# A DiT attention block: the shift of channels 256 to 1151 computed as rows by column-tiled matmuls and turned by one VectorE block transpose

## The chip, the cores and the metric

The kernel runs on one core of one Trainium2 chip, in one launch. The metric is device time in microseconds (us), the median of several runs. A profiled execution stands beside it: its span is the time from the first to the last instruction, and its own time has what lies around the span as well.

## The reference

B = 2 batches of N = 256 tokens, D = 1152 channels, all arrays bf16. Cut to what matters:

```python
mod = (_silu(c) @ w_mod).reshape(B, 6, 1, D)
shift_a, scale_a, gate_a, shift_m, scale_m, gate_m = [mod[:, i] for i in range(6)]
h = _layernorm(x, axis=-1) * (1 + scale_a) + shift_a
qkv = h @ wqkv
q, k, v = ...                      # thirds of qkv
p = _softmax(jnp.einsum('bqd,bkd->bqk', q, k) * D ** (-0.5), axis=-1)
a = jnp.einsum('bqk,bkd->bqd', p, v) @ wo
return x + gate_a * a
```

Only shift_a, scale_a and gate_a are used. Each is one row of 1152 numbers per batch: silu(c), 2 x 1152, times 1152 columns of w_mod.

## The kernel before, in words

Channels and tokens. The 512 tokens of both batches (T) are handled together. h is kept transposed, with channels on partitions, in nine blocks of 128 channels: hT_sb[:, cc, :] is 128 channels by 512 tokens. The query and key projections contract over channels, so block k of hT_sb is the moving operand of the matmuls for block k, and the weights' 128 x 128 tiles are stationary. The shift is wanted in the same form: a scalar per partition for each block and batch, sh_sb[:, cc, b].

How shift and scale are made. scT_sb holds silu(c) transposed: 128 partitions by 9 blocks by 32 columns, of which two are the batches and thirty are zero. mod_mm (L489) takes, for each channel block cc, nine matmuls: a 128 x 128 tile of w_mod stationary, two columns of scT_sb moving. The result, 128 channels by 2 batches, adds up in PSUM bank 7 (ps[7]). s_mm / s_ev (L497, L500) do this for the scale by the groups in SGROUPS, h_mm / h_ev (L506, L509) for the shift by HGROUPS = [(0, 3), (3, 6), (6, 9)], 27 matmuls a group. h_ev copies 6 columns from PSUM into sh_sb on VectorE, and shift_group (L667) then adds the shift to each block and batch of the group (shift_x, L529): of every three such instructions two go to VectorE (DVE) and the third to GpSimd (POOL).

How the gate is made (L779). Here silu(c) is stationary, 32 columns of scT_sb, and 288 columns of w_mod move. Four such matmuls stand side by side on column tiles of the array, and write to partitions 0, 32, 64 and 96 of one bank. Nine rounds of four add up over the channels of c. The result are rows, one per batch.

Order of the work. The program is a list of operations; each engine works off its own part in the order in which they are listed, and waits are worked out from what reads and writes what. PSUM banks count as a whole: an engine that touches a bank waits for the last use by each other engine. PE's order around the change is:

- Keys, seven output blocks at a time (j = 0 to 6, banks 0 to 6), for channel blocks k = 0 to 8. h0T_sb (stored in pvT_sb) holds the scaled blocks that they need. In the loop over groups after L652 the scale matmuls of the next group, s_mm(g + 1), are listed after the seven matmuls of the first block of a group (k = 4 for g = 2), and scale_group(g + 1) (L628) puts the eviction s_ev and the scalings on DVE (batch 0) and POOL (batch 1) behind them. After k = 6 stands rep (L470), after k = 7 h_mm(0).
- The two remaining key blocks ("kb"), on banks 7 and 0.
- Queries, seven output blocks on banks QB = [1, 2, 3, 4, 5, 6, 0], by HGROUPS and k (L687): after the seven matmuls of the first k of a group the next group's shift is listed, h_mm(g + 1), h_ev(g + 1), shift_group(g + 1). So h_mm(1) stands after k = 0, and h_mm(2) after k = 3.
- The two remaining query blocks ("qb"), values with scores between (L722, L735), the gate, the product of probabilities and values (L800), the output projection (L838).

Loads. SP issues nearly all of them, in one queue and in listed order: x, scale groups of w_mod ("s"), key weights ("ka") by channel blocks, then shift group 0 (L291), kb, and in turns the query weights of three channel blocks (L294, 128 x 3 x 896) and the next shift group, then qb and the value weights. wm_sb is one buffer: w_mod's gate columns (L702) later take the place of the scale groups, and wo (L704) that of the shift groups, after their last matmul.

Of the kernel before, what the change touches and what calls it, by code (L numbers as in the profile page):

```python
# [10 lines left out]
PE = mybir.EngineType.PE  # L11
DVE = mybir.EngineType.DVE
# [9 lines left out]
class _Prog:  # L22
# [12 lines left out]
    def op(self, eng, fn, r=(), w=(), dma=False, extra=()):  # L35
        o = _Op()
        o.eng, o.fn, o.dma = eng, fn, dma
        o.sem = o.val = None
        o.inc = False
        deps = set(extra)  # L40
        for k in r:
            if k[0] == "ps":
                continue
            p = self.last_w.get(k)
            if p is not None and not (p.eng == eng == PE):
                deps.add(p)
            self.readers.setdefault(k, []).append(o)
        for k in w:
            if k[0] == "ps":
                continue  # L50
            for q in self.readers.get(k, ()):
                if q is not o and (q.dma or dma or q.eng != eng):
                    deps.add(q)
            p = self.last_w.get(k)
            if p is not None and p is not o and not (p.eng == eng == PE):
                deps.add(p)
            self.readers[k] = [o] if k in r else []
            self.last_w[k] = o
        for k in set(r) | set(w):
            if k[0] != "ps":  # L60
                continue
            accesses = self.bank.setdefault(k, {})
            for e, q in accesses.items():
                if e != eng:
                    deps.add(q)
            accesses[eng] = o
        deps.discard(o)
        o.deps = deps
        self.ops.append(o)
        return o  # L70
# [73 lines left out]
D = 1152  # L144
T = B * NTOK
P = 128
DC = D // P
# [4 lines left out]
CONST_B = 0.0294189453125  # L152

SGROUPS = [(0, 2), (2, 4), (4, 6), (6, 9)]
HGROUPS = [(0, 3), (3, 6), (6, 9)]
NA = 7
EARLY = 5
GW = 288
# [39 lines left out]
def _build(nc, es, x, c, wqkv, wo, w_mod, out):  # L198
    bf16 = dt.bfloat16
    f32 = dt.float32  # L200
# [8 lines left out]
    sb = lambda name, shape, dtype: es.enter_context(nc.sbuf_tensor(name, list(shape), dtype))  # L209
# [7 lines left out]
    wm_sb = sb("wm_sb", [P, 2 * DC * D], bf16)  # L217
# [20 lines left out]
    rc_sb = sb("rc_sb", [P, DC, 2], f32)  # L238
    scT_sb = sb("scT_sb", [P, DC, 32], bf16)
    s1_sb = sb("s1_sb", [P, DC, 2], f32)  # L240
    sh_sb = sb("sh_sb", [P, DC, 2], f32)
    gaterow_sb = sb("gaterow_sb", [P, GW], bf16)
    stat_sb = sb("stat_sb", [P, TT, 5, 3], f32)
    mv_sb = sb("mv_sb", [P, TT, 2], f32)
# [10 lines left out]
    ps = [es.enter_context(nc.psum_tensor(f"psbank{i}", [P, 512], f32)) for i in range(8)]  # L255
# [3 lines left out]
    op = pg.op  # L259
# [5 lines left out]
    h_off = []  # L265
    for a, b_ in HGROUPS:
        h_off.append(off)
        off += DC * (b_ - a) * P

    def wm_ap(o, w):  # L270
        return bass.AP(wm_sb, o, [[2 * DC * D, P], [w, DC], [1, w]])

    def s_ap(g):
        return wm_ap(s_off[g], (SGROUPS[g][1] - SGROUPS[g][0]) * P)

    def h_ap(g):
        return wm_ap(h_off[g], (HGROUPS[g][1] - HGROUPS[g][0]) * P)

# [10 lines left out]
    def load_h(g):  # L289
        a, b_ = HGROUPS[g]  # L290
        op(SP, lambda e: e.dma_start(h_ap(g), wm_v[:, :, a * P:b_ * P]), w=[("wh", g)], dma=True)  # L291

    def load_w(tag, k0, k1, c0, c1):
        op(SP, lambda e: e.dma_start(wq_sb[:, k0:k1, c0:c1], wq_v[:, k0:k1, c0:c1]),  # L294
           w=[("w", tag, k) for k in range(k0, k1)], dma=True)
# [13 lines left out]
    pg.tag = None  # L309
    load_h(0)  # L310
    load_w("kb", 0, DC, D + NA * P, 2 * D)
    for g, (a, b_) in enumerate(HGROUPS):
        if g:
            load_h(g)
        load_w("qa", a, b_, 0, NA * P)
    load_w("qb", 0, DC, NA * P, D)
    for k0 in range(0, DC, 3):
        load_w("v", k0, k0 + 3, 2 * D, 3 * D)
# [170 lines left out]
    def mod_mm(src, keys, a, b_, col, base):  # L489
        for cc in range(a, b_):  # L490
            for k in range(DC):
                op(PE, lambda pe, cc=cc, k=k: pe.matmul(  # L492
                    ps[7][:, col + 2 * cc:col + 2 * cc + 2], src[:, k, (cc - base) * P:(cc - base + 1) * P],
                    scT_sb[:, k, 0:2], start=(k == 0), stop=(k == DC - 1)),
                   r=keys + [("scT",)], w=[("ps", 7), ("mr", col, cc)])

    def s_mm(g):  # L497
        mod_mm(s_ap(g), [("ws", g)], *SGROUPS[g], 0, SGROUPS[g][0])

    def s_ev(g):  # L500
        a, b_ = SGROUPS[g]
        src = ps[7][:, 2 * a:2 * b_].rearrange("p (c b) -> p c b", b=2)
        op(DVE, lambda v: v.tensor_scalar(s1_sb[:, a:b_, :], src, 1.0, None, op0=ALU.add),  # L503
           r=[("ps", 7)] + [("mr", 0, cc) for cc in range(a, b_)], w=[("s1", cc) for cc in range(a, b_)])

    def h_mm(g):  # L506
        mod_mm(h_ap(g), [("wh", g)], *HGROUPS[g], 64, HGROUPS[g][0])

    def h_ev(g):  # L509
        a, b_ = HGROUPS[g]  # L510
        src = ps[7][:, 64 + 2 * a:64 + 2 * b_].rearrange("p (c b) -> p c b", b=2)
        op(DVE, lambda v: v.tensor_copy(sh_sb[:, a:b_, :], src),
           r=[("ps", 7)] + [("mr", 64, cc) for cc in range(a, b_)], w=[("sh", cc) for cc in range(a, b_)])

    h0T_sb = pvT_sb

    def scale_x(cc, tiles, eng):
        lo, hi, b = tiles[0] * P, (tiles[-1] + 1) * P, tiles[0] // 2
        dst, src, sc = h0T_sb[:, cc, lo:hi], xnT_sb[:, cc, lo:hi], s1_sb[:, cc, b:b + 1]
        rk = [("xnT", cc, i) for i in tiles] + [("s1", cc)]  # L520
        wk = [("h0", cc, i) for i in tiles]
        if eng == DVE:
            op(DVE, lambda v: v.tensor_scalar(dst, src, sc, None, op0=ALU.mult), r=rk, w=wk)
        elif eng == POOL:
            op(POOL, lambda g: g.tensor_scalar(dst, src, sc, 0.0, op0=ALU.mult, op1=ALU.add), r=rk, w=wk)  # L525
        else:
            op(AC, lambda a: a.activation(dst, src, ACT.Copy, scale=sc), r=rk, w=wk)
# [13 lines left out]
    def qk_mm(tag, src, key, col, k, bank, tiles=(0, 1, 2, 3), start=None):  # L541
        lo, hi = tiles[0] * P, (tiles[-1] + 1) * P
        rk = [(key, k, i) for i in tiles] if key == "h0" else [(key, k, b) for b in range(B)]
        op(PE, lambda pe: pe.matmul(ps[bank][:, lo:hi], wq_sb[:, k, col * P:(col + 1) * P],  # L544
                                    src[:, k, lo:hi], start=(k == 0) if start is None else start,
                                    stop=(k == DC - 1), skip_group_check=True),
           r=[("w", tag, k)] + rk, w=[("ps", bank)])
# [18 lines left out]
    for t in ORDER:  # L566
        pg.tag = t
        n, args = t[0], t[1:]
# [18 lines left out]
        elif n == "e1":  # L587
            op(AC, lambda a: a.activation(e1_sb[:, :, :], cT_sb[:, :, :], ACT.Exp, scale=-1.0),
               r=[("cT",)], w=[("e1",)])
# [5 lines left out]
        elif n == "scT":  # L595
            op(POOL, lambda g: g.tensor_tensor(scT_sb[:, :, 0:2], cT_sb[:, :, :], rc_sb[:, :, :], ALU.mult),
               r=[("cT",), ("rc",)], w=[("scT",)])
# [24 lines left out]
    def center_group(g):  # L622
        a, b_ = SGROUPS[g]
        for cc in range(a, b_):
            for b in CENTRED:
                center(cc, (2 * b, 2 * b + 1), DVE)

    def scale_group(g):  # L628
        s_ev(g)
        a, b_ = SGROUPS[g]  # L630
        for cc in range(a, b_):
            for b in range(B):
                scale_x(cc, (2 * b, 2 * b + 1), POOL if b == 1 else DVE)
        if g + 1 < len(SGROUPS):
            center_group(g + 1)
# [13 lines left out]
    for g in range(2, len(SGROUPS)):  # L649
        a, b_ = SGROUPS[g]  # L650
        for k in range(a, b_):
            for j in range(NA):  # L652
                qk_mm("ka", h0T_sb, "h0", DC + j, k, j)
            if k == a and g + 1 < len(SGROUPS):
                s_mm(g + 1)
                scale_group(g + 1)
            b = k - 6
            if b in CENTRED:
                rep(b)
                rep_out(b)  # L660
                for cc in range(0, 6):
                    norm_x(cc, b)
            if k == DC - 2:
                h_mm(0)
    h_ev(0)

    def shift_group(g):  # L667
# [29 lines left out]
    for n, bank in enumerate((7, 1)):  # L697
# [5 lines left out]
       w=[("wgate",)] + [("ws", g) for g in range(len(SGROUPS))], dma=True)  # L703
    op(SP, lambda e: e.dma_start(wo_ap, wo_v),  # L704
       w=[("wo",)] + [("wh", g) for g in range(len(HGROUPS))], dma=True)
# [71 lines left out]
    for k in range(DC):  # L777
        for j in range(4):
# [3 lines left out]
               r=[("wgate",), ("scT",)], w=[("ps", bank)])  # L782
    op(AC, lambda a, bank=bank: a.activation(gaterow_sb[:, :], ps[bank][:, 0:GW], ACT.Copy),
       r=[("ps", bank)], w=[("grow",)])
    for b in range(B):
        for j in range(4):
            row = bass.AP(gaterow_sb, (32 * j + b) * GW, [[GW, 1], [0, P], [1, GW]])
            op(SP, lambda e, b=b, j=j, row=row: e.dma_start(gate_rep[:, b, j * GW:(j + 1) * GW], row),
               r=[("grow",)], w=[("gate", b, j)], dma=True)
# [38 lines left out]
    for i in range(TT):  # L828
        b = i // 2
        cols = [(0, 384), (384, 768), (768, 1152)] if i < TT - 1 else [  # L830
            (0, 384), (384, 768), (768, 1024), (1024, 1152)]
        for (c0, c1) in cols:
            n = c1 - c0
            bank = next_bank()
            gated = i == TT - 1 and c0 >= LC
            for k in range(DC):
                rhs = wog_ap[:, k, c0 - LC:c1 - LC] if gated else wo_ap[:, k, c0:c1]
                op(PE, lambda pe, i=i, k=k, rhs=rhs, n=n, bank=bank: pe.matmul(  # L838
                    ps[bank][:, 0:n], pvT_sb[:, k, i * P:(i + 1) * P], rhs,
                    start=(k == 0), stop=(k == DC - 1)),  # L840
                   r=[("pv", k, b), ("wog", k) if gated else ("wo",)], w=[("ps", bank)])
            if gated:
                op(DVE, lambda v, i=i, c0=c0, c1=c1, n=n, bank=bank: v.tensor_tensor(  # L843
                    xo_sb[:, i, c0:c1], ps[bank][:, 0:n], x_sb[:, i, c0:c1], ALU.add),
                   r=[("ps", bank), ("x", i)], w=[("o", i, c0)])
# [7 lines left out]
               r=[("ps", bank)] + gk, w=[("ga", s)])  # L853
            op(DVE, lambda v, i=i, c0=c0, c1=c1, n=n, s=s: v.tensor_tensor(  # L854
                xo_sb[:, i, c0:c1], x_sb[:, i, c0:c1], ga_sb[:, s, 0:n], ALU.add),
               r=[("x", i), ("ga", s)], w=[("o", i, c0)])
# [38 lines left out]
```

## Time and profile before

| | us |
|---|---|
| median of 6 runs | 99.02 |
| lowest, highest | 98.63, 100.28 |
| the profiled execution, its own time | 98.7 |
| its span | 96.9 |

The profile names engines: PE is TensorE's matmuls, PEld its weight loads (which overlap PE), DVE VectorE, ACT ScalarE, POOL GpSimd, SP the engine that issues loads. A group line gives the line of the kernel, engine, operation, what is written and read, and a count. psbank is any PSUM bank. PE's granted clock is full in all slices. In the prediction times are us from the start of the span.

### The profile page before, as it was taken

The page shows a single profiled execution, that of the slowest core. Times are in us where ns is not written, and L with a number is a line of the kernel's source. Part 1 is how long each engine was busy: PE and PEld are TensorE (multiplying, and loading weights), DVE is VectorE, ACT ScalarE, POOL GpSimd, SP SyncE. Part 2 cuts the span into 40 slices and gives each one's busy share as a digit, 9 for nine tenths or more (in the row PEclk, how much of TensorE's full clock was granted, in tenths as well). Part 3 has the DMA queues.
Part 4 walks back from the last instruction along what each step waited for, and adds up shares of the span by engine and source line. Part 5 has one row for each costly group of instructions (what it writes and reads, how often), then busy time and mean ns, then how long its engine had stood idle before and what let it go on. Part 6 is the DMA issues. An engine that isn't in the chain of part 4 may idle for free.

```text
span 96.9 us, 1890 instructions
## 1 busy us (share of the span) xinstructions
PE 92.4 (95%) x765; PEld 56.7 (59%) x765; DVE 47.9 (49%) x136; ACT 28.5 (29%) x64; POOL 12.7 (13%) x36
## 2 busy tenths in 40 slices
PE   5996999999999999999999999999999999999990
PEld 1375877655644646444456786566658856666670
DVE  1486860830999040503620266452026737799571
ACT  2795869911050200002322223622224800000000
POOL 4016451563030040400000000000000000000000
PEclk9999999999999999999999999999999999999999
DMA  2999999999999999999999971125675656121222
GB/s 29 366 309 317 365 318 342 359 338 309 354 337 360 338 343 346 389 392 394 391 391 392 394 299 49 29 52 24 27 52 48 39 42 100 48 81 41 84 79 81
DMA packets 21244, 21.91 MB, mean 226 GB/s; under 512 B 2034, under 2 KB 17266, under 8 KB 21236
## 3 DMA queue, kind: packets, MB, share of 16 engines
q1 hardware_dynamic: 21088, 21.50, 76.6%
q10 hardware_dynamic: 148, 0.30, 0.9%
q8 instruction: 6, 0.10, 0.4%
q14 instruction: 2, 0.02, 0.0%
HBM read 19.76 MB, written 1.18 MB: 216 GB/s over the span
## 4 chain that ended last, share of the span: by engine, by line
PE 88%; DMA 7%; SPq 1%; ACT 1%; issue 1%; DVE 0%
PE psbank L544 36%; PE psbank L722 18%; PE psbank L838 18%; DMA wm_sb<-in_w_mod_dram 7%; PE psbank L492 4%; PE psbank L735 4%; PE psbank L800 4%; SPq L283 1%; PE psbank L779 1%; PE psbank L394 1%; ACT xnT_sb L341 1%; PE psbank L475 0%; DVE xo_sb L843 0%
## 5 line engine op out<-in xcount | busy, mean ns | idle before, releaser
L544 PE MATMUL psbank<-pvT_sb,wq_sb 128*128 128x512 bf16 (+2 forms) x111 | 18.4, 321 | 0.0
L722 PE MATMUL psbank<-wq_sb,hT_sb 128*128 128x384 bf16 x108 | 18.1, 326 | 0.0
L544 PE MATMUL psbank<-hT_sb,wq_sb 128*128 128x512 bf16 x81 | 18.0, 379 | 0.0
L838 PE MATMUL psbank<-wm_sb,pvT_sb 128*128 128x384 bf16 x99 | 16.3, 326 | 0.0
L722 PEld LDWEIGHTS psbank<-wq_sb,hT_sb 128*128 128x128 bf16 x108 | 10.5, 98 | 7.1 <-DVE v_sb L339 0.2
L544 PEld LDWEIGHTS psbank<-pvT_sb,wq_sb 128*128 128x128 bf16 x111 | 9.6, 97 | 6.7 <-POOL pvT_sb L525 0.3
L838 PEld LDWEIGHTS psbank<-wm_sb,pvT_sb 128*128 128x128 bf16 x99 | 9.7, 98 | 6.3
L544 PEld LDWEIGHTS psbank<-hT_sb,wq_sb 128*128 128x128 bf16 x81 | 7.8, 98 | 9.1
L341 ACT ACTIVATE qkT_sb<-psbank 128x512 bf16<-128x512 f32 x8 | 4.3, 598 | 22.3 <-PE psbank L544 22.3
L339 DVE CAST qkT_sb<-psbank 128x512 bf16<-128x512 f32 x10 | 6.3, 683 | 5.6 <-PE psbank L544 5.6
L339 DVE CAST v_sb<-psbank 128x384 bf16<-128x384 f32 x6 | 3.2, 554 | 11.8 <-PE psbank L722 11.8
L851 DVE TENSOR_TENSOR ga_sb<-psbank,gate_rep 128x384 bf16<-128x384 f32 x11 | 6.1, 555 | 4.1 <-PE psbank L838 4.1
L492 PEld LDWEIGHTS psbank<-scT_sb,wm_sb 128*128 128x128 bf16 x162 | 4.9, 96 | 2.0 <-POOL nmr_sb L374 1.0
L492 PE MATMUL psbank<-scT_sb,wm_sb 128*128 128x2 bf16 x162 | 5.0, 163 | 0.8 <-DMA wm_sb<-in_w_mod_dram 0.8
L341 ACT ACTIVATE v_sb<-psbank 128x384 bf16<-128x384 f32 x6 | 2.9, 487 | 9.3 <-PE psbank L722 9.3
L525 POOL TENSOR_SCALAR pvT_sb<-xnT_sb,s_sb 128x256 bf16<-128x256 bf16 (+1 forms) x9 | 5.0, 564 | 3.2 <-DVE s_sb L503 2.8
L333 PE MATMUL psbank<-warm_sb 128*128 128x512 bf16 x9 | 4.2, 628 | 1.2 <-DVE warm_sb L321 1.2
L486 DVE TENSOR_TENSOR hT_sb<-pvT_sb,rep_sb 128x256 bf16<-128x256 bf16 x9 | 3.2, 419 | 2.9 <-ACT rep_sb L480 2.9
L854 DVE TENSOR_TENSOR xo_sb<-x_sb,ga_sb 128x384 bf16<-128x384 bf16 x11 | 3.9, 358 | 0.4
L735 PE MATMUL psbank<-qkT_sb 128*128 128x256 bf16 x36 | 4.1, 272 | 0.0
L800 PE MATMUL psbank<-pT_sb,v_sb 128*128 128x256 bf16 x36 | 4.1, 272 | 0.0
L735 PEld LDWEIGHTS psbank<-qkT_sb 128*128 128x128 bf16 x36 | 3.5, 98 | 0.5
(82 smaller groups left out, 79.5 us busy)
## 6 DMA issues: line engine op xcount, KB each, us to landing
wm_sb<-in_w_mod_dram SPq DMA_DIRECT2D x4, 864.0 KB, 9.7
wq_sb<-in_wqkv_dram SPq DMA_DIRECT2D x4, 672.0 KB, 10.0
wq_sb<-in_wqkv_dram SPq DMA_DIRECT2D x3, 864.0 KB, 10.7
wm_sb<-in_w_mod_dram SPq DMA_DIRECT2D x1, 2592.0 KB, 15.8
wm_sb<-in_wo_dram SPq DMA_DIRECT2D x1, 2592.0 KB, 20.5
wm_sb<-in_w_mod_dram SPq DMA_DIRECT2D x3, 576.0 KB, 7.1
wq_sb<-in_wqkv_dram SPq DMA_DIRECT2D x2, 576.0 KB, 10.3
out_dram<-xo_sb SPq DMA_DIRECT2D x11, 96.0 KB, 1.6
```

The lines of the kernel that those rows point to most:

```text
L333: op(PE, lambda pe: pe.matmul(ps[bank][:, 0:512], warm_sb[:, 0:P], warm_sb[:, 0:512], start=True, stop=True), r=[("warm",)], w=[("ps", bank)])
L339: op(DVE, lambda v: v.tensor_copy(dst, src), r=r, w=w)
L341: op(AC, lambda a: a.activation(dst, src, ACT.Copy), r=r, w=w)
L492: op(PE, lambda pe, cc=cc, k=k: pe.matmul(ps[7][:, col + 2 * cc:col + 2 * cc + 2], src[:, k, (cc - base) * P:(cc - base + 1) * P], scT_sb[ ...
L525: op(POOL, lambda g: g.tensor_scalar(dst, src, sc, 0.0, op0=ALU.mult, op1=ALU.add), r=rk, w=wk)
L544: op(PE, lambda pe: pe.matmul(ps[bank][:, lo:hi], wq_sb[:, k, col * P:(col + 1) * P], src[:, k, lo:hi], start=(k == 0) if start is None el ...
L722: op(PE, lambda pe, k=k, q=q, bank=bank: pe.matmul(ps[bank][:, 0:384], hT_sb[:, k, i * P:(i + 1) * P], wq_sb[:, k, 2 * D + q * 384:2 * D + ...
L735: op(PE, lambda pe, cc=cc: pe.matmul(ps[bank][:, 0:NTOK], qkT_sb[:, cc, i * P:(i + 1) * P], qkT_sb[:, DC + cc, b * NTOK:(b + 1) * NTOK], s ...
L800: op(PE, lambda pe, h=h, cc=cc, sbk=sbk: pe.matmul(ps[bank][:, h * NTOK:(h + 1) * NTOK], v_sb[:, 2 * b + sbk, cc * P:(cc + 1) * P], pT_sb[ ...
L838: op(PE, lambda pe, i=i, k=k, rhs=rhs, n=n, bank=bank: pe.matmul(ps[bank][:, 0:n], pvT_sb[:, k, i * P:(i + 1) * P], rhs, start=(k == 0), s ...
L851: op(DVE, lambda v, b=b, c0=c0, c1=c1, n=n, bank=bank, s=s: v.tensor_tensor(ga_sb[:, s, 0:n], ps[bank][:, 0:n], gate_rep[:, b, c0:c1], ALU ...
L854: op(DVE, lambda v, i=i, c0=c0, c1=c1, n=n, s=s: v.tensor_tensor(xo_sb[:, i, c0:c1], x_sb[:, i, c0:c1], ga_sb[:, s, 0:n], ALU.add), r=[("x ...
```

## The change

Channel blocks 0 and 1 keep the old way. For blocks 2 to 8 the shift is computed as the gate is: scT_sb[:, k, :] (32 columns) stationary, w_mod's shift columns moving, four column tiles side by side. Tile j takes columns 32 j to 32 j + 31 of each of the seven blocks, 224 columns in all, so its moving operand is strided: runs of 32 columns, 128 apart. Nine rounds of four fill 128 partitions x 224 of bank 7; row 32 j + b of 32-column piece c holds batch b's shift for channels 32 j to 32 j + 31 of block a + c. One VectorE transpose of 32 x 32 blocks reads this from PSUM and writes it to sh_sb, which now has 32 columns per block, of which the first two are used. It takes the place of the copies of two groups.

HGROUPS becomes [(0, 2), (2, 9)]: 18 narrow matmuls in h_mm(0), and the whole rest as h_mm(1), after the query matmuls of k = 0; fourteen shift_x instructions follow it. The loads are put in another order: shift 0 (2 blocks), kb, query weights of block 0, shift 1 (7 blocks, 2016 KB), query weights of block 1, of 2 to 4, of 5 to 8. Last, s_mm(3) and its scale_group are listed after the second matmul of k = 5 instead of the seventh of k = 4.

```diff
-HGROUPS = [(0, 3), (3, 6), (6, 9)]
+HGROUPS = [(0, 2), (2, 9)]
...
-    sh_sb = sb("sh_sb", [P, DC, 2], f32)
+    sh_sb = sb("sh_sb", [P, DC, 32], f32)
...
-    for g, (a, b_) in enumerate(HGROUPS):
-        if g:
-            load_h(g)
-        load_w("qa", a, b_, 0, NA * P)
+    load_w("qa", 0, 1, 0, NA * P)
+    load_h(1)
+    load_w("qa", 1, 2, 0, NA * P)
+    load_w("qa", 2, 5, 0, NA * P)
+    load_w("qa", 5, 9, 0, NA * P)
...
     def h_mm(g):
-        mod_mm(h_ap(g), [("wh", g)], *HGROUPS[g], 64, HGROUPS[g][0])
+        a, b_ = HGROUPS[g]
+        if g == 0:
+            mod_mm(h_ap(g), [("wh", g)], a, b_, 64, a)
+            return
+        n = b_ - a
+        for k in range(DC):
+            for j in range(4):
+                rhs = bass.AP(wm_sb, h_off[g] + k * n * P + 32 * j, [[2 * DC * D, P], [P, n], [1, 32]])
+                op(PE, lambda pe, k=k, j=j, rhs=rhs: pe.matmul(
+                    ps[7][32 * j:32 * (j + 1), 0:32 * n].rearrange("p (c r) -> p c r", c=n), scT_sb[:, k, :], rhs,
+                    start=(k == 0), stop=(k == DC - 1)),
+                   r=[("wh", g), ("scT",)], w=[("ps", 7), ("mr", 64, a)])
...
     def h_ev(g):
         a, b_ = HGROUPS[g]
-        src = ps[7][:, 64 + 2 * a:64 + 2 * b_].rearrange("p (c b) -> p c b", b=2)
-        op(DVE, lambda v: v.tensor_copy(sh_sb[:, a:b_, :], src),
-           r=[("ps", 7)] + [("mr", 64, cc) for cc in range(a, b_)], w=[("sh", cc) for cc in range(a, b_)])
+        wk = [("sh", cc) for cc in range(a, b_)]
+        if g == 0:
...
+        op(DVE, lambda v: v.transpose(sh_sb[:, a:b_, :].rearrange("p c r -> p (c r)"), ps[7][:, 0:32 * (b_ - a)]),
+           r=[("ps", 7), ("mr", 64, a)], w=wk)
...
-            if k == a and g + 1 < len(SGROUPS):
-                s_mm(g + 1)
-                scale_group(g + 1)
+                if j == 1 and k == b_ - 1 and g + 1 < len(SGROUPS):
+                    s_mm(g + 1)
+                    scale_group(g + 1)
```

More of the change, by code (lines that the diff above doesn't have):

```diff
@@ L506, in h_mm @@
     def h_mm(g):
-        mod_mm(h_ap(g), [("wh", g)], *HGROUPS[g], 64, HGROUPS[g][0])
+        a, b_ = HGROUPS[g]
[10 more added lines that the diff above has]
+                   r=[("wh", g), ("scT",)], w=[("ps", 7), ("mr", 64, a)])
     def h_ev(g):
         a, b_ = HGROUPS[g]
-        src = ps[7][:, 64 + 2 * a:64 + 2 * b_].rearrange("p (c b) -> p c b", b=2)
-        op(DVE, lambda v: v.tensor_copy(sh_sb[:, a:b_, :], src),
-           r=[("ps", 7)] + [("mr", 64, cc) for cc in range(a, b_)], w=[("sh", cc) for cc in range(a, b_)])
+        wk = [("sh", cc) for cc in range(a, b_)]
+        if g == 0:
+            src = ps[7][:, 64 + 2 * a:64 + 2 * b_].rearrange("p (c b) -> p c b", b=2)
+            op(DVE, lambda v: v.tensor_copy(sh_sb[:, a:b_, 0:2], src),
+               r=[("ps", 7)] + [("mr", 64, cc) for cc in range(a, b_)], w=wk)
+            return
+        op(DVE, lambda v: v.transpose(sh_sb[:, a:b_, :].rearrange("p c r -> p (c r)"), ps[7][:, 0:32 * (b_ - a)]),
+           r=[("ps", 7), ("mr", 64, a)], w=wk)
     h0T_sb = pvT_sb
```

## The prediction

> **What bounds the kernel now.** I read the table of engines first, then the slices, then the chain that ended last, then single instructions, and last the loads. The page, engines and slices (busy tenths of 2.4 us each):
>
> ```profile
> PE 92.4 (95%) x765; PEld 56.7 (59%) x765; DVE 47.9 (49%) x136; ACT 28.5 (29%) x64; POOL 12.7 (13%) x36
> ...
> PE   5996999999999999999999999999999999999990
> ...
> DVE  1486860830999040503620266452026737799571
> ...
> DMA  2999999999999999999999971125675656121222
> ```
>
> TensorE (PE) has work in every slice from the second on; DVE has half of its time free. The DMA engines are full to about 56 us, so loads are a second limit in the first half. The chain that ended last, in order of time (start us, us, what):
>
> ```profile
> 19.80 0.68 PE psbank L492 x27
> 20.49 3.04 PE psbank L544 x14
> ...
> 25.38 0.65 PE psbank L492 x27
> 26.03 6.93 PE psbank L544 x32
> 32.96 0.65 PE psbank L492 x27
> 33.61 4.55 PE psbank L544 x21
> 38.17 0.65 PE psbank L492 x27
> 38.82 11.46 PE psbank L544 x53
> ...
> 62.99 1.22 PE psbank L779 x36
> ```
>
> After 10.57 us the chain has only matmuls on it, one block straight after the other, to the last. So a microsecond less on PE between 25 and 39 us is a microsecond less at the end, if nothing else comes late. The three shift blocks are the L492 x27 at 25.38, 32.96 and 38.17; the one at 19.80 belongs to the scale. L779 x36 is the gate: the only column-tiled matmuls here, of the very form that the change adds. The edges of one shift block and of the gate, matmul by matmul (start us, duration us):
>
> ```profile
> 32.58 0.38 PE L544 MATMUL psbank<-hT_sb,wq_sb 128*128 128x512 bf16 x1
> 32.80 0.17 PE L492 MATMUL psbank<-scT_sb,wm_sb 128*128 128x2 bf16 x1
> 33.45 0.16 PE L492 MATMUL psbank<-scT_sb,wm_sb 128*128 128x2 bf16 x1
> 33.48 0.38 PE L544 MATMUL psbank<-hT_sb,wq_sb 128*128 128x512 bf16 x1
> ```
> ```profile
> 62.66 0.33 PE L722 MATMUL psbank<-wq_sb,hT_sb 128*128 128x384 bf16 x1
> 62.92 0.30 PE L779 MATMUL psbank<-wm_sb,scT_sb 128*32 128x288 bf16 x1
> ...
> 64.14 0.34 PE L722 MATMUL psbank<-wq_sb,hT_sb 128*128 128x384 bf16 x1
> ```
>
> Durations contain the latency of the array, so prices are taken from starts. 512-column matmuls start 0.216 us apart; after the one at 32.58 another could have started at 32.80, but starts at 33.48. One block costs 33.48 - 32.80 = 0.68 us, 25.2 ns for each of 27. For the gate, the matmul at 62.66 (384 columns) streams to 62.82; the next ordinary one starts at 64.14: 1.32 us. In it the rounds of four start 0.121 us apart (62.92, 63.05, 63.17 and so on), 9 x 0.121 = 1.09 us; what is left, 0.22 us, is the change of tiling on both sides.
>
> What follows a shift block on DVE:
>
> ```profile
> 33.65 0.17 DVE L512 COPY sh_sb<-psbank 128x6 f32<-128x6 f32 x1 [2.38 <-PE psbank L492]
> 33.85 0.29 DVE L535 TENSOR_SCALAR hT_sb<-hT_sb,sh_sb 128x256 bf16<-128x256 bf16 x1
> 34.05 0.51 DVE L535 TENSOR_SCALAR hT_sb<-pvT_sb,sh_sb 128x256 bf16<-128x256 bf16 x1
> ```
>
> The bracket says that DVE had idled 2.38 us and waited for PE: it is free when the shift comes.
>
> **What the Trainium skill says.** TensorEngine Tiling (Array Packing), Key Properties: a change of tiling mode drains TensorE, while tiles within a mode work in parallel. The trace agrees: 0.22 us at the edges of the gate, and four 288-column matmuls in 0.121 us, which is 288 columns once (the ordinary matmul takes 0.216 / 512 = 0.422 ns a column, 0.1215 us for 288). TensorE: Matmul & The Clock Gate, Back-to-back issue gap: 1 to 64 columns cost a floor of about 25 ns; the trace has 25.2. For the new operation, VectorE: DVE Perf Modes, The three transpose paths: a VectorE transpose works in 32x32 blocks and takes 311 ns for 128x128 bf16. No VectorE transpose is in the trace of before.
>
> **The change, part by part.**
>
> *Narrow matmuls removed.* Group 0 shrinks from 27 to 18: -9 x 25.2 ns = -0.23 us. The blocks at 32.96 and 38.17 go: -2 x 0.68 = -1.36. All of it lies on the chain: -1.59 us.
>
> *Column-tiled pass added, after the seven query matmuls of k = 0.* Nine rounds of four with 7 x 32 = 224 columns: 224 x 0.422 = 0.0945 us a round, 0.85 us, and 0.22 us for the change of tiling: 1.07 us, on the chain. Its reads differ from the gate's: runs of 32 columns, 128 apart. Lower bound 0.95 (the edges cost half), upper bound the gate's 1.32; beyond that is a rival below. I take 1.07, because the gate's rounds match their streaming time so closely.
>
> *Eviction.* Two copies of 0.165 us become one transpose of 224 f32 columns from PSUM. Nearest rows: the L339 casts from f32 PSUM, 681 ns for 512 columns and 557 for 384, 0.97 ns a column and 185 fixed: 0.40 us for 224; the skill's 311 ns for 128 columns is in line with that. Bounds 0.25 to 0.70 (double the slope is 0.62). Cover: PE goes on with the seven matmuls of k = 1, whose shift is in group 0: 7 x 0.216 = 1.51 us, before k = 2 needs channel block 2. The times of after: the pass begins 0.23 us earlier, at 32.57, and ends at 33.64; its last matmul started some 0.2 us before and ends, with the latency of 0.17, near 33.70; transpose 33.74 to 34.14; first shift at 34.17, second at 34.37, done at 34.65 to 34.88 (L535 took 0.28, and 0.51 when POOL worked beside it). PE wants block 2's matmul at 33.64 + 1.51 = 35.15 and its weight load some 0.2 earlier, at 34.95. Margin 0.1 to 0.3 us for 0.40, so the cost is nil; with 0.70 up to 0.2 us would show. Behind the waiting transpose on DVE are only the ten shifts of its group; POOL has four, 0.57 us each beside DVE (L537). Each further k needs one block in 1.51 us while DVE and POOL need some 0.7: they run away from PE.
>
> *Loads on the SP queue.* Landing times (issue plus time to landing, from the DMA view): scale group 3 19.6, key weights 6 to 8 21.4, shift 0 24.2, "kb" 26.1, query 0 to 2 27.9, shift 1 30.5, query 3 to 5 32.4, shift 2 35.15, query 6 to 8 37.0. That is 5184 KB in 15.6 us, 333 KB/us; the 896-column loads alone went at 672 KB in 1.86 us, 361. The new order with 333: shift 0 (576 KB) 23.2, kb 24.9, query 0 (224) 25.6, shift 1 (2016) 31.7, query 1 32.3, query 2 to 4 34.3, query 5 to 8 37.0. Needed: shift 1 at 32.57, query 1 at 33.6, query 2 at 35.0 for its weight load. Slack 0.9, 1.3 and 0.7 us, and about 0.5 more each if wide rows go at 361. I take nil; later loads keep their bytes and order. The wo load (L704) now waits for the pass at 33.6, not for the block at 38.2.
>
> *Scale group 3 two matmuls later.* Its 27 matmuls move from after k = 4 to 0.43 us later. PE's weight load had waited there 0.35 us for this load, which landed as PE became free (19.66 against 19.65), so 0.02 us is saved here and there is room if it is late. In return DVE's scale (L503) comes at 20.95, not 20.53, while POOL is in its own small steps to 21.24 either way, and then makes block 6, which PE waits for:
>
> ```profile
> 21.80 0.10 PEld L544 LDWEIGHTS psbank<-pvT_sb,wq_sb 128*128 128x128 bf16 x1 [0.28 <-POOL pvT_sb L525]
> 21.86 0.38 PE L544 MATMUL psbank<-pvT_sb,wq_sb 128*128 128x512 bf16 x1
> ```
>
> That matmul starts on time, with next to no room. DVE's own scalings now fall beside POOL's first (0.48 alone, 0.57 beside DVE): up to 0.1 us of stall. Net +0.02, bounds -0.1 to +0.1.
>
> **Sum.** -1.59 + 1.07 + 0.02 = -0.50 us. Against the profiled execution (span 96.9, its own time 98.7, 1.8 around the span) this gives 98.2; the median shown is 0.3 above that execution, so 99.02 - 0.50 = 98.5. The unknowns (pass 0.95 to 1.32, scale step -0.1 to +0.1) give 98.3 to 98.85.
>
> **The rivals.**
>
> *The tiles get into each other's way: slower.* The gate's four tiles read 576 bytes apart, the new ones 64 bytes apart in runs of 64 bytes. If they can't be fed side by side, the rounds stretch. It decides from a pass of 1.59 us, a round of (1.59 - 0.22) / 9 = 0.152 us against 0.0945. Two at a time: 9 x 0.189 + 0.22 = 1.92 us, 99.02 + 0.33 = 99.35; one at a time 3.62 us, 101.05. For it: no strided moving operand in the trace. Against: the run is as long as the whole 64 bytes, and four readers at once are shown by the gate. Price taken: 99.4.
>
> *The wait only moves.* One transpose over everything makes block 2 late, or POOL makes block 6 late, and PE pays 0.2 to 0.5 us at 35 or at 21.9: about 98.85. For it: margins of 0.1 to 0.3 us. Against: DVE is idle before the transpose.
>
> *The big shift load is late.* 2016 KB must land whole, and its end stands 3392 KB behind the key weights, where the old shift 1's stood 2976. If it lands at 33.0, PE idles 0.4 us and about 98.9 results; it is slower than before from a landing at 33.07. For it: DMA is full. Against: 0.9 us of slack at the mean rate.
>
> That the change doesn't do what it says can be left aside: the order of PE's instructions in the changed program has 18 narrow matmuls and then one pass of 36 in these places.
>
> **How the numbers follow.** The forecast has 0.65 (of it 0.48 faster by over 0.5%, that is below 98.52, and 0.17 within); the tiles 0.11, slower; the moved wait 0.15 (0.13 within, 0.02 slower); the late load 0.09 (0.06 within, 0.03 slower). 0.5% is about what a measurement of this kernel can tell from no change. Faster 0.48, within 0.36, slower 0.16. The range goes from 98.1 (pass 0.95, scale step -0.1, and 0.15 for the spread of a median) to 99.1, which takes in the moved wait and most late loads and leaves out the tiles' case.
>
> **What would show it.** Right: the next ordinary matmul starts 1.0 to 1.15 us after the last one before the pass has streamed, rounds 0.095 apart; a transpose of about 0.4 us; no idle time of PE at k = 2; the last output 0.5 us earlier. Wrong: rounds of 0.12 us or more, PE waiting for hT_sb near 35 us, for pvT_sb near 21.9, or for a load near 32.6.

## The result, and the profile after

| | before | after |
|---|---|---|
| median, us | 99.08 (69 runs) | 98.37 (34 runs) |
| lowest, us | 98.57 | 98.05 |
| profiled execution: own time, span | 98.7, 96.9 | 98.73, 96.9 |

Some executions of every kernel take about 1.5% longer or more, many of them with a mean granted clock of 0.983; the medians count them, the ratios and intervals leave them out, and the two profiled executions of this kind (without the move the second time, with late loads without the move) are read closely only in the last section.

The ratio of after to before is 0.9927, 95% interval 0.991 to 0.9944: 0.7 us less, where 0.5 was forecast. Yet the two profiled executions took the same time. Whoever compares only these two spans would say that nothing happened; the chain says why. The chain of after, in order of time (start us, us, what):

```profile
9.94 10.45 DMA wm_sb<-in_w_mod_dram
...
20.44 0.83 PE psbank L493 x27
21.27 1.10 PE psbank L561 x5
...
22.38 1.67 PE psbank L561 x7
24.05 0.34 PE psbank L476 x6
...
25.89 0.43 PE psbank L493 x18
26.32 6.93 PE psbank L561 x32
33.25 0.98 PE psbank L516 x36
34.23 16.08 PE psbank L561 x74
...
94.65 0.29 DVE xo_sb L860
```

The chain now starts on PE only at 20.44; before that it is the load of scale group 3, which left at 9.94 and landed at 20.4. In the execution of before it landed at 19.6. This one load came 0.8 us later, although all that is issued before it is the same, and that hid the gain. So the two traces have to be compared from a common point on: the first key matmul of block 6 (at 21.86 before, at 22.38 after), behind which PE has no gap. The chain of before ends with

```profile
94.63 0.29 DVE xo_sb L843
```

From block 6 to the start of the last output instruction it is 94.63 - 21.86 = 72.77 us before and 94.65 - 22.38 = 72.27 after: 0.50 us less.

The edges of the shift's pass in after, from the timeline (start us, duration us, operation):

```profile
32.87 0.38 PE L561 MATMUL psbank<-hT_sb,wq_sb 128*128 128x512 bf16 x1
33.18 0.28 PE L516 MATMUL psbank<-wm_sb,scT_sb 128*32 128x224 bf16 x3
33.96 0.27 PE L516 MATMUL psbank<-wm_sb,scT_sb 128*32 128x224 bf16 x4
34.16 0.39 PE L561 MATMUL psbank<-hT_sb,wq_sb 128*128 128x512 bf16 x1
```

The ordinary matmul at 32.87 streams to 33.09, the next one starts at 34.16: 1.07 us. First and last round start 0.78 apart; by their starts in the trace the second round begins 0.106 us after the first, and the others follow 0.096 apart (0.0975, as texts below have it, is 0.78 / 8). And the eviction in after, DVE's timeline and then PE's weight loads (in brackets how long the engine idled, and what ended it):

```profile
34.28 0.42 DVE L529 STREAM_TRANSPOSE sh_sb<-psbank 128x224 f32<-128x224 f32 x1 [2.68 <-PE psbank L516]
34.73 0.29 DVE L552 TENSOR_SCALAR hT_sb<-hT_sb,sh_sb 128x256 bf16<-128x256 bf16 x1
34.94 0.51 DVE L552 TENSOR_SCALAR hT_sb<-pvT_sb,sh_sb 128x256 bf16<-128x256 bf16 x1
```
```profile
35.50 0.10 PEld L561 LDWEIGHTS psbank<-hT_sb,wq_sb 128*128 128x128 bf16 x1 [0.15 <-DVE hT_sb L552]
```

The weight load of query block 2 is 0.15 us late and its matmul still on time: PE's starts run on at 0.216 us through 35.47, 35.68 and 35.90.

### The profile page after: what moved, and what is told of

Its sections match the earlier page's. It is cut to its first block, busy times and chain, and to the rows that moved or that the text cites. A ratio compares the mean times of both kernels' runs of the same rounds, so it can differ in the third digit from the quotient of the medians.

```text
span 96.9 us, 1836 instructions
## 1 busy us (share of the span) xinstructions
PE 92.1 (95%) x738; PEld 55.7 (57%) x738; DVE 48.2 (50%) x136; ACT 28.5 (29%) x64; POOL 12.3 (13%) x35
## 4 chain that ended last, share of the span: by engine, by line
PE 77%; DMA 11%; SPq 9%; issue 1%; DVE 0%
PE psbank L561 28%; PE psbank L739 18%; PE psbank L855 18%; DMA wm_sb<-in_w_mod_dram 11%; SPq L294 6%; PE psbank L817 4%; PE psbank L752 4%; SPq L287 2%; PE psbank L493 1%; SPq L283 1%; PE psbank L796 1%; PE psbank L516 1%; PE psbank L476 0%; DVE xo_sb L860 0%
## 5 line engine op out<-in xcount | busy, mean ns | idle before, releaser
L493 PE MATMUL psbank<-scT_sb,wm_sb 128*128 128x2 bf16 x99 | 3.2, 163 | 1.1 <-DMA wm_sb<-in_w_mod_dram 1.1
L493 PEld LDWEIGHTS psbank<-scT_sb,wm_sb 128*128 128x128 bf16 x99 | 3.0, 96 | 2.0 <-DMA wm_sb<-in_w_mod_dram 1.0
L817 PEld LDWEIGHTS psbank<-pT_sb,v_sb 128*128 128x128 bf16 x36 | 3.5, 98 | 0.5
## 6 DMA issues: line engine op xcount, KB each, us to landing
wm_sb<-in_wo_dram SPq DMA_DIRECT2D x1, 2592.0 KB, 22.4
```

The costliest lines, as they stand in the source:

```text
L493: op(PE, lambda pe, cc=cc, k=k: pe.matmul(ps[7][:, col + 2 * cc:col + 2 * cc + 2], src[:, k, (cc - base) * P:(cc - base + 1) * P], scT_sb[ ...
L817: op(PE, lambda pe, h=h, cc=cc, sbk=sbk: pe.matmul(ps[bank][:, h * NTOK:(h + 1) * NTOK], v_sb[:, 2 * b + sbk, cc * P:(cc + 1) * P], pT_sb[ ...
```

## The experiments

Three theories stood against each other for the 0.2 us that the sum didn't have. A: they come from the move of scale group 3, because block 6 waits for the later of two loads. B: the pass alone is worth 0.7 us. C: the new load order is. All kernels were timed beside the kernel before; a ratio is to that kernel, with its 95% interval, and 0.001 of it is 0.1 us.

**The move alone.** Edit, on the kernel before:

```diff
-            if k == a and g + 1 < len(SGROUPS):
-                s_mm(g + 1)
-                scale_group(g + 1)
+                if j == 1 and k == b_ - 1 and g + 1 < len(SGROUPS):
+                    s_mm(g + 1)
+                    scale_group(g + 1)
```

> The kernel before with one edit: the matmuls of scale group 3 listed two key matmuls later. Theory A (the gain above the 0.50 us of the sum comes from this move: key block 6 starts at the later of two times, scale group 3's landing + 0.7 + the key matmuls behind it, or the landing of its key weights + 0.1; before, the first is 0.25 us later than the second): 0.15 to 0.3 us faster than before, about 98.85, and block 6 starts 0.1 us after the landing of key weights 6 to 8. Theory B (the swap of the matmuls alone is worth 0.7 us): no difference. Theory C (the new load order is worth the rest): no difference.

Measured: 98.80 us, ratio 0.9982 (0.9952 to 1.0012); the sign of A, within the noise. In the trace scale group 3 landed at 9.81 + 9.7 = 19.51, key weights 6 to 8 at 10.54 + 10.8 = 21.34, and block 6 started at 21.49, 0.15 after the latter, as A has it. From there to the last output 94.25 - 21.49 = 72.76, as before.

**All but the move.** The reverse of that edit, on the changed kernel. It ran twice, the second time beside the changed kernel.

> The changed kernel with scale group 3's matmuls back at their old place. Theory A: 0.50 us faster than before and 0.2 us slower than the changed kernel, about 98.6. Theory B and theory C: like the changed kernel, 98.4.

> The changed kernel with scale group 3's matmuls at their old place, a second time beside the changed kernel. Theory A: 0.15 to 0.3 us slower than the changed kernel; block 6 starts 2.2 us after scale group 3's landing and 0.4 us after that of key weights 6 to 8. Theory B (the move is worth nothing): the same time as the changed kernel within 0.1 us.

Measured: 98.39 us, ratio 0.9931 (0.9897 to 0.9965), and 98.58, 0.9955 (0.993 to 0.9979). Block 6 in the first trace: scale group 3 landed at 9.94 + 9.7 = 19.64, key weights at 10.67 + 10.8 = 21.47, and block 6 started at 20.39 + 7 x 0.2155 = 21.90, 2.26 after the one and 0.43 after the other, as A has it; from there to the end 94.17 - 21.90 = 72.27. So the mechanism of A is in the trace, but its size in the medians is less than expected.

**The changed kernel again**, as the neighbour.

> The changed kernel once more, as the neighbour on the same chip for the three below: about 98.4. In the trace PE works 72.27 us from the first key matmul of block 6 to the last output, whatever the loads did before it, and block 6 starts 0.1 us after the landing of key weights 6 to 8 if theory A is right.

Measured: 98.52 us, ratio 0.9945 (0.9918 to 0.9972), against 0.9955 for its neighbour without the move: 0.1 us faster. That is less than A's 0.15 to 0.3 and at the edge of B's "same within 0.1", but each interval reaches 0.25 us to either side, so the times exclude neither. Block 6 started at 22.53, key weights had landed at 22.4; to the end 72.27.

**Narrow matmuls for all blocks**, with the groups, loads and move of the change:

```diff
     def h_mm(g):
         a, b_ = HGROUPS[g]
-        if g == 0:
-            mod_mm(h_ap(g), [("wh", g)], a, b_, 64, a)
-            return
...
+        mod_mm(h_ap(g), [("wh", g)], a, b_, 64, a)
     def h_ev(g):
...
-        op(DVE, lambda v: v.transpose(sh_sb[:, a:b_, :].rearrange("p c r -> p (c r)"), ps[7][:, 0:32 * (b_ - a)]),
+        op(DVE, lambda v: v.tensor_copy(sh_sb[:, a:b_, 0:2], src),
```

> The changed kernel with channel blocks 2 to 8 computed by 63 narrow matmuls and one copy, no column tiles, no transpose; groups, load order and move as changed. PE has 63 x 25.2 ns = 1.59 us where the pass has 1.07. Theory A: 0.5 us slower than the changed kernel, 0.2 faster than before, about 98.85. Theory B: like before, 99.1. Theory C: between, like theory A, but then the run with the move alone shows no gain.

Measured: 98.83 us, ratio 0.9985 (0.9968 to 1.0002), and 94.73 - 21.97 = 72.76 us from block 6 to the end. Groups, load order and move together are worth at most 0.3 us. C is out: the new load order takes nothing from the path (72.76 with it, 72.77 before), and the 0.50 us are the pass. The times say the same: the changed kernel, with its ratios of 0.9927 and 0.9945, is 0.4 to 0.6 us faster than this one.

**Key weights in two loads**, on the changed kernel:

```diff
-    ('s', 3), ('w', 6, 9),
+    ('s', 3), ('w', 6, 7), ('w', 7, 9),
```

> The changed kernel with the load of key weights 6 to 8 issued as two loads, block 6 and blocks 7 and 8. Theory A: after the change this load's landing is what block 6 waits for; with a third of its bytes it lands 1.1 us earlier, and scale group 3's landing decides again: 0.1 to 0.2 us faster than the changed kernel, about 98.2, and block 6 starts 1.8 us after scale group 3's landing. Theories B and C: like the changed kernel, 98.4.

Measured: 98.27 us in 7 runs, ratio 0.992 (0.9891 to 0.995): not apart from the changed kernel. In its profiled execution PE was late for another reason (1.1 us of waiting for x_sb, L395), scale group 3 had landed long before it was needed, and block 6 started right behind the key matmuls. It tells nothing on A.

**The transpose twice**, to measure the room behind it:

```diff
-        op(DVE, lambda v: v.transpose(sh_sb[:, a:b_, :].rearrange("p c r -> p (c r)"), ps[7][:, 0:32 * (b_ - a)]),
-           r=[("ps", 7), ("mr", 64, a)], w=wk)
+        for _ in range(2):
+            op(DVE, lambda v: v.transpose(sh_sb[:, a:b_, :].rearrange("p c r -> p (c r)"), ps[7][:, 0:32 * (b_ - a)]),
+               r=[("ps", 7), ("mr", 64, a)], w=wk)
```

> The changed kernel with the VectorE transpose done twice, one after the other, the second over the same output. It measures the room left by the seven matmuls of query block 1. The trace of the changed kernel has the weight load of block 2 at 35.50, 0.15 us late, its matmul on time at 35.68. Theory A: 0.42 us more on VectorE puts block 2 about 0.27 us late and the end as much: 98.65. Rival (the cover is wide, as the copies before had it): no change, 98.4.

Measured: 98.81 us, ratio 0.9978 (0.9951 to 1.0006), 0.29 above its neighbour of the same chip (ratio 0.9945); the two intervals overlap at their ends, so the trace has to decide. Its weight loads and matmuls:

```profile
35.38 0.55 PEld L562 LDWEIGHTS psbank<-hT_sb,wq_sb 128*128 128x128 bf16 x4 [0.60 <-DVE hT_sb L553]
```
```profile
35.38 0.39 PE L562 MATMUL psbank<-hT_sb,wq_sb 128*128 128x512 bf16 x1
```

The pass had ended with the ordinary matmul at 33.59, so this one was due at 33.59 + 7 x 0.2155 = 35.10: 0.28 late. From 33.59 to the last output it is 60.77 us, where the changed kernel has 94.65 - 34.16 = 60.49. Of 0.42 us more on DVE 0.28 came through, so the transpose has 0.14 us of room.

**Smaller loads ahead of block 6**, a version meant to be faster, on the changed kernel:

```diff
-SGROUPS = [(0, 2), (2, 4), (4, 6), (6, 9)]
+SGROUPS = [(0, 2), (2, 4), (4, 6), (6, 8), (8, 9)]
...
-    ('s', 3), ('w', 6, 9),
+    ('s', 3), ('w', 6, 7), ('s', 4), ('w', 7, 9),
...
-                scale_x(cc, (2 * b, 2 * b + 1), POOL if b == 1 else DVE)
+                scale_x(cc, (2 * b, 2 * b + 1), (AC if cc == 6 else POOL) if b == 1 else DVE)
...
-                if j == 1 and k == b_ - 1 and g + 1 < len(SGROUPS):
+                if j == 1 and k == (5, 6, 9)[g - 2] and g + 1 < len(SGROUPS):
```

> The changed kernel with the loads ahead of block 6 made smaller: scale group 3 is blocks 6 and 7, a new group 4 is block 8; key weights 6 to 8 come as block 6, then scale group 4, then blocks 7 and 8; scale group 4's matmuls stand after the second key matmul of block 6; batch 1 of block 6 is scaled by ACT in place of POOL. Theory A: the waits of PE for scale group 3 and for key weights before block 6 (0.5 and 0.17 us in the profile of after) go: 0.2 to 0.6 us faster than the changed kernel, 97.8 to 98.2. Theory B: as the changed kernel. Against it: group 4's rows are 256 bytes, and key weights 7 and 8 may land late.

> The version with smaller loads ahead of block 6 once more, for its interval: 0.2 to 0.5 us faster than the changed kernel, 97.9 to 98.3, if the waits for loads before block 6 cost every execution something; like the changed kernel, 98.4, if they cost only the profiled one.

Measured: 98.18 us in 9 runs, ratio 0.9913 (0.9881 to 0.9945), and 98.73 in 22 runs, ratio 0.9923 (0.9894 to 0.9952). In the first PE's wait for scale group 3 was gone, and the output came at 93.99; in the second x had kept PE 0.7 us behind before (L395), and it came at 94.75. The intervals lie over those of the changed kernel: no better version is shown.

**Late loads, without and with the move**, on the changed kernel:

```diff
+    dum_sb = sb("dum_sb", [P, D], bf16)
...
-    ('s', 3), ('w', 6, 9),
+    ('dum',), ('s', 3), ('w', 6, 9),
...
+        elif t[0] == "dum":
+            op(SP, lambda e: e.dma_start(dum_sb[:, :], x_pi[:, 0, :]), w=[("dum",)], dma=True)
```

> The changed kernel with scale group 3's matmuls at their old place, and with one more load of 288 KB (x tile 0 again, into an unused buffer) on the SP queue ahead of scale group 3, so that this group and key weights 6 to 8 land some 0.85 us later in every execution. Theory A (the move is worth min(lateness, 0.3) us, where lateness is how long PE would wait for scale group 3): block 6 starts 2.25 us after group 3's landing, and the kernel is 0.25 to 0.3 us slower than its neighbour with the move. Theory B (the move is worth nothing): both the same.

> The changed kernel, scale group 3's matmuls at their new place, with the same additional load of 288 KB. Theory A: block 6 starts 0.1 us after the landing of key weights 6 to 8, which is 1.95 us after group 3's: 0.25 to 0.3 us faster than its neighbour without the move, about 0.6 us slower than the changed kernel. Theory B: as its neighbour.

Measured: without the move 99.58 us, ratio 1.0026 (0.9995 to 1.0056); with it 99.08, 1.0005 (0.9961 to 1.0049). The move's sign again; 0.5 us between the medians and 0.2 between the ratios, but the intervals overlap. A's start of block 6 without the move can't be read, because the clock fell in that profiled execution. With the move, key weights landed at 22.4 (11.45 + 10.9), block 6 started at 22.52, and the end came 72.27 later.

**Neighbouring columns for the tiles**, on the changed kernel:

```diff
-                rhs = bass.AP(wm_sb, h_off[g] + k * n * P + 32 * j, [[2 * DC * D, P], [P, n], [1, 32]])
+                rhs = bass.AP(wm_sb, h_off[g] + k * n * P + 32 * n * j, [[2 * DC * D, P], [32, n], [1, 32]])
```

> The changed kernel with each tile of the pass reading 224 neighbouring columns (tiles 448 bytes apart, as in the gate) in place of seven runs of 32, 128 apart. This changes which channel a shift value goes to, so part of the computation is another one. If the strided reads of four tiles hinder each other (the rival of the prediction, in a mild form), rounds shrink from the 0.0975 us of after to the 0.0945 of streaming and the pass by 0.03 us; if the reads are free, nothing changes: rounds 0.0975, pass 1.07, about 98.4.

Measured: 98.39 us, ratio 0.9938 (0.9908 to 0.9968). Its pass:

```profile
32.20 0.38 PE L561 MATMUL psbank<-hT_sb,wq_sb 128*128 128x512 bf16 x1
32.51 1.05 PE L516 MATMUL psbank<-wm_sb,scT_sb 128*32 128x224 bf16 x36
33.49 0.39 PE L561 MATMUL psbank<-hT_sb,wq_sb 128*128 128x512 bf16 x1
```

From 32.20 + 0.216 = 32.42 to 33.49 it is 1.07 us, with rounds 0.096 apart as in after: these strided reads cost nothing.

## Why the prediction was right, and where it was off

*The swap of matmuls: right to the hundredth.* Forecast -1.59 + 1.07. In after the 18 narrow ones take from 25.73 to 26.18, 0.45 us where 27 took 0.68, and the pass 1.07. Inside the pass two errors of 0.01 us cancel: the prediction read the gate's rounds as 0.121 apart, where after the first they start 0.1225 apart, so that its edges are 0.21 and not 0.22; and the rounds of the pass take 0.096, not 0.0945. The sum of the PE path shows without any noise of loads: 72.77 us from block 6 to the end in the three traces with narrow matmuls (before, 72.76 with the move alone and with all-narrow groups), 72.27 in after, in its repetition, without the move, with late loads and the move, and with neighbouring columns. 0.50 us, wherever the move stood. B's 0.7 for the pass is out.

*The tiles' rival: out.* Rounds of 0.096 us where streaming would be 0.0945; the contiguous form has the same.

*The eviction: right, and with little to spare.* 0.42 us for the transpose where 0.40 was taken, DVE idle before it. The 0.40 had been worked out from another operation, the casts; no line of before showed that a transpose goes at their rate, so part of this hit is luck. The cover held with 0.14 us left, inside the 0.1 to 0.3 forecast; the doubled transpose shows that this rival starts where it was said to.

*The loads of the shift: right.* The 2016 KB were issued at 22.54 and landed 9.3 later, at 31.84 (forecast 31.7); the pass didn't start before 33.18. This rival is not far off, though: in the first run with smaller loads PE came to the pass earlier, the load landed at 32.39, and the pass started at 32.52, 0.15 us later behind the matmul before it than in after.

*The move of scale group 3: mis-sized.* Forecast +0.02, bounds -0.1 to +0.1, because in the trace of before this group lands as PE comes free. That was one execution. The step compared the load with PE only, and not with the other load that block 6 needs. Over the traces the key weights land 1.8 to 1.9 us after the group; with the old order block 6 starts 2.25 us after the group's landing if PE had to wait for it, with the new one 0.1 to 0.15 after the key weights', that is about 2.0. If the group comes d late, the old order loses d, the new one d - 0.27 or nothing: the move is worth the smaller of d and 0.27 us. It is worth nothing where the group is in time, as in the trace of before. It landed between 19.5 and 20.6 in the traces with the same loads up to it, so the value changes from run to run. The ratios give, with the move against without: -0.1 us beside each other, -0.2 on the kernel before, and -0.2 with late loads. All have one sign, none is clear of its interval; the traces show the mechanism, and the size stays open between nothing and some 0.2 us. Nor was the feared stall by POOL found. Before block 6, the wait of PE's weight load in after is put down to POOL, but POOL's instruction for block 6 ended at 22.14:

```profile
22.35 0.77 PEld L561 LDWEIGHTS psbank<-pvT_sb,wq_sb 128*128 128x128 bf16 x5 [0.47 <-POOL pvT_sb L542]
```
```profile
21.57 0.57 POOL L542 TENSOR_SCALAR pvT_sb<-xnT_sb,s_sb 128x256 bf16<-128x256 bf16 x1 [0.69 <-DVE s_sb L504]
```

The key weights were issued at 10.67 and took this long to land (last number, us):

```profile
wq_sb<-in_wqkv_dram SPq DMA_DIRECT2D x1, 672.0 KB, 11.6
```

That is 22.2 to 22.3, and the weight load came 0.1 us behind it. In two traces (key weights in two loads, transpose twice) the key weights came early enough that POOL did end last, 0.05 us before the weight load, and the matmul of block 6 still started on time.

*The whole.* -0.50 from the pass and about -0.1 to -0.2 from the move make -0.6 to -0.7, where 0.71 was measured with an interval from 0.55 to 0.89, and 0.54 (0.28 to 0.81) in the repetition. What is left lies within the noise.

## What to carry to other kernels

When PE is busy without a gap, price an exchange of matmuls from the starts of its neighbours, and take the price of a form from a place where the kernel already uses it; here this was right to 0.01 us. Compare two traces from the last point at which a load decided, not from their beginnings: two equal spans hid half a microsecond here. Where an instruction needs several loads, write each one's landing plus the work behind it side by side; an order that takes work from behind the last load helps just until the next load is the later one.

## What the runs showed of the hardware

A VectorE 32x32-block transpose of 128 x 224 f32 from PSUM took 0.42 us, where the two nearest rows of plain evicting copies gave an estimate of 0.40 for this size: by that estimate it is hardly dearer than a copy. Changing to column tiles and back cost 0.21 us in the gate (1.31 - 9 x 0.1225) and the same in the pass (1.07 - 9 x 0.096).

Two profiled executions show something that the others don't. Without the move, second time: PE waited 1.71 us for x at 7.15. Its timeline, and then its busy time by stretch (from and to in us of the span, us long, PE busy and count, granted clock, DMA share, GB/s):

```profile
7.15 1.38 PE L395 MATMUL psbank<-ident,x_sb 128*128 128x128 bf16 x18 [1.71 <-DMA x_sb<-in_x_dram]
```
```profile
0.00:6.00 6.00, 4.26 (x18) 1.00 0.64 196
6.00:9.00 3.00, 1.66 (x22) 0.92 1.09 312
9.00:11.00 2.00, 1.77 (x31) 0.50 1.14 308
11.00:13.00 2.00, 2.00 (x22) 0.50 0.98 335
13.00:15.00 2.00, 2.00 (x30) 0.50 1.14 323
15.00:19.00 4.00, 4.00 (x38) 0.96 1.08 346
```

With late loads, no move: PE waited 1.7 us for scale group 3, and the same table has:

```profile
19.20:21.30 2.10, 0.42 (x2) 1.00 1.11 341
22.00:25.00 3.00, 3.00 (x15) 0.50 1.15 283
25.50:26.50 1.00, 1.00 (x6) 1.00 1.02 363
```

Both times the granted clock fell to half within 1.5 us after the wait, and stayed there for 3 us or more while PE was busy. It costs time: with late loads the fourteen key matmuls of blocks 5 and 6 took 26.36 - 22.03 = 4.33 us from the first start to the last, where before has 23.15 - 20.35 = 2.80. In the other traces, with waits of at most 1.1 us in these stages, the clock stayed full (mean 0.999 or 1.000). The Trainium skill (TensorE: Matmul & The Clock Gate, What's actually happening) describes a gate that halves the clock after an idle window of about 3.4 us; the halving agrees, but here the longest single waits before it were 1.7 us, and the measurement decides. That the waits caused the fall is not shown: there are two such executions, and no run put such a wait in on purpose. With late loads, a wait of 1.7 us thus stood beside another 1.5 us lost to the lower clock, which is a reason to take waits for loads out even where the median shows little.
